# Halves of q and k in an attention kernel: copies by ScalarE, VectorE and GpSimd in place of transfers within SBUF, and another order of the work

## The chip, the cores and the metric

The kernel runs on one core of a Trainium2 chip. The core has TensorE (PE in the profile: matmuls, with PEld for its weight loads), VectorE (DVE), ScalarE (ACT), GpSimd (POOL) and SyncE (SP), which here issues all DMAs; 16 DMA queues move data between HBM, where inputs and outputs lie, and SBUF, the working memory of 128 partitions ("rows" below). Matmuls write to PSUM, here seven buffers of 128x512 f32 and one for the running state. The metric is the device time of one execution in microseconds (us); lower is better.

## The reference

Inputs q, k and v are 4 x 8 x 768 x 64 (batch, heads, sequence, head size). First a retention with decay, then a mixture of four causal attentions over its output, of which each token takes the two with the highest gate:

```python
for t in range(S):
    state = gamma[None, :, None, None] * state + np.einsum('bhd,bhe->bhde', k[:, :, t], v[:, :, t])
    y[:, :, t] = scale * np.einsum('bhd,bhde->bhe', q[:, :, t], state)
...
logits = x @ w_gate
topk = np.argpartition(-logits, K, axis=-1)[..., :K]
...
for e in range(E):
    q = x @ wq[e]
    k = x @ wk[e]
    v = x @ wv[e]
    scores = scale * (q @ k.transpose(0, 2, 1))
    scores = np.where(causal, -1000000000.0, scores)
    scores = scores - scores.max(-1, keepdims=True)
    a = np.exp(scores)
    a /= a.sum(-1, keepdims=True) + 1e-09
    ye = a @ v @ wo[e]
    for kk in range(K):
        mask = topk[:, :, kk] == e
        out += mask[..., None] * w[:, :, kk:kk + 1] * ye
```

Here x is the retention's output as 4 x 768 x 512, and E = 4, K = 2.

## The kernel before

**Stages.** The sequence of each batch is cut into 6 chunks of 128 tokens (24 in all, index g) for the retention, and into 2 halves of 384 tokens (8 in all, index j) for the attention.

- *Retention* (`h1`, `h2`, `kdecay`, `qdecay`; matmuls of lines 477, 481, 536, 542): 64x64 matmuls for four pairs of heads, two heads at a time on the upper and lower 64 rows. Each chunk's q and k come with one load of 512 KB (`qkT_t`, three buffers), k and v in the other layout with a second one (`kv_t`, three buffers). A buffer is free for the next load when the chunk's matmuls and decays are done. The result is split into a rounded part `xh` (ACT) and a rest `xl` (DVE).
- *Projection* (`proj`, lines 577 to 616): for a half j, a pair of experts p and an expert e of it, twelve matmuls (line 592) give q in rows 0 to 63 and k in rows 64 to 127 of one PSUM buffer, 384 tokens wide. ACT takes the rounded part into `k1` (line 597), DVE the rest into `q2` (line 600). Then transfers within SBUF place the parts: the high part of q in both row halves of `q1`, the low part of k in the upper half of `k1` over its high part in the lower half, and the high part of k in the upper half of `k2`. Experts come in pairs, so a transfer holds 64 rows of 2 x 384 values, 192 KB; in the last half (j = 7) each expert has its own, 96 KB.
- *Row maxima* (`mpass`, lines 715 to 737, and `mrow`), *values and gate* (`vgate`, line 634, `gate`, `gate2`).
- *Attention* (`score`, lines 841 and 842): k1 against q1 in 128 rows is (k low + k high) times q high, and k2 against q2 adds k high times q low and, in row 64, the row maximum. ACT takes the exponential into `pt` (line 848), POOL masks the diagonal (line 854) and adds up the denominators (lines 863, 870); `av` (line 889) multiplies with v.
- *Norm and output* (`norm_a`, `norm_b`, `norm_last`, `wout`, line 1015).

**What sets the order.** Each step is recorded by `op` with its engine and what it reads and writes. `ORDER`, a table of numbers, then gives the order in which all steps are written out, and so the order on each engine's queue: engines work their queues in order, and SP issues DMAs in order too, waiting at each for what it depends on. Buffers of a tag are handed out in that order as well. The costs that stand beside the steps now only pick which of a tag's free buffers a step gets.

At the head, `warm` (line 1153) gives PE eight 128x512 matmuls on a tile of zeros, and `idle` (line 1163) six more at two places.

Of the kernel before, what the change touches and what calls it, by code (L numbers as in the profile page):

```python
# [8 lines left out]
F32 = mybir.dt.float32  # L9
# [18 lines left out]
WARM = 8  # L28
IDLE = (2, 4)
# [69 lines left out]
"""  # L99


def act_c(n):
    return 0.17 + n * 0.83e-3


def dve_c(n):
    return 0.15 + n * 1.04e-3
# [140 lines left out]
def tile_retention_moe_attention(  # L248
# [328 lines left out]
    def proj(j, p, e):  # L577
# [35 lines left out]
        for x, rows_ in (("a", up), ("b", low)):  # L613
            move(q1, rows_, k1, up, [(k1, "q", y) for y in es], [(q1, x, y) for y in es])
# [678 lines left out]
```

## Time and profile before

Three runs took 337.05, 338.60 and 338.72 us.

| | |
|---|---|
| median of the runs | 338.60 us |
| the profiled execution's own time | 337.56 us |
| its span in the profile | 335.9 us |
| mean granted clock of TensorE | 0.995 |
| HBM read, written | 29.99 MB, 6.79 MB |
| SP's instructions for moves within SBUF (line 609) | 56 of 192 KB, 16 of 96 KB |

The page gives each engine's busy time, then the span in 40 slices, where each digit is the busy share of a slice in tenths:

```profile
PE   7869979988996799999999999999999999999995
DVE  3832736666624434645664627575634446668753
ACT  2323223421531443244353432353354514547631
POOL 5554322562383695377056894535088733627200
PEclk9999999999997999999999999999999999999999
DMA  7955756654728506565663864442164040443012
```

One slice is 8.4 us. "Idle before" in a group's row is the time in which the engine stood still just ahead of such an instruction, with what ended it; "issue" is idle time that the profile gives no reason for. The chain of waits follows the work that ended last back to the start.

### The profile page before, as it was taken

The numbers are of one execution on the slowest core, as the hardware profiler recorded it, in microseconds if no ns is written. First come the engines' busy times: TensorE is split into PE (matmuls) and PEld (weight loads), VectorE is DVE, ScalarE is ACT, GpSimd is POOL, SyncE is SP. The second block draws the span as 40 slices with busy tenths as digits, with TensorE's granted clock in tenths as the row PEclk, the third lists the DMA queues.
The fourth block names the chain that finished last, engine by engine and source line by source line (L and its number), as shares of the span: only waits on it lengthen the run. The fifth ranks groups of instructions, "written<-read, shape, count | busy, mean of one in ns | idle before, by whom it ended". The sixth has DMA issues, their size and how long they took to land.

```text
span 335.9 us, 11897 instructions
## 1 busy us (share of the span) xinstructions
PE 315.6 (94%) x5060; PEld 278.9 (83%) x5060; DVE 181.2 (54%) x506; ACT 129.0 (38%) x322; POOL 169.0 (50%) x192
## 2 busy tenths in 40 slices
PE   7869979988996799999999999999999999999995
PEld 4669979877985797998999979998998979987773
DVE  3832736666624434645664627575634446668753
ACT  2323223421531443244353432353354514547631
POOL 5554322562383695377056894535088733627200
PEclk9999999999997999999999999999999999999999
DMA  7955756654728506565663864442164040443012
GB/s 264 399 198 182 203 174 198 176 178 158 188 83 237 173 5 193 167 221 146 195 201 91 257 180 136 140 112 88 50 173 100 23 124 24 135 118 91 33 66 95
DMA packets 21642, 50.15 MB, mean 149 GB/s; under 512 B 3186, under 2 KB 8390, under 8 KB 21588
## 3 DMA queue, kind: packets, MB, share of 16 engines
q1 hardware_dynamic: 21588, 49.38, 48.5%
q8 instruction: 40, 0.66, 0.8%
q14 instruction: 14, 0.11, 0.1%
HBM read 29.99 MB, written 6.79 MB: 110 GB/s over the span
## 4 chain that ended last, share of the span: by engine, by line
PE 92%; issue 4%; DMA 1%; DVE 1%; ACT 0%; SPq 0%; ACTq 0%
PE ps L592 20%; PE ps L889 11%; PE ps L634 11%; PE ps L1015 10%; PE ps L841 7%; PE ps L842 6%; PE ps_st L477 5%; PE ps L542 5%; PE ps L729 4%; PE ps L536 3%; PE ps L481 2%; PE ps L715 2%; PE ps L925 2%; DMA qkT_t<-in_qkT_dram 1%; PE ps L728 1%
## 5 line engine op out<-in xcount | busy, mean ns | idle before, releaser
L854 POOL TENSOR_SCALAR_AFFINE_SELECT pt<-pt 128x256 f32<-128x256 f32 x48 | 20.1, 423 | 81.2 <-ACT pt L848 81.0
L848 ACT ACTIVATE pt<-ps 128x384 f32<-128x384 f32 (+2 forms) x112 | 49.4, 494 | 23.8 <-PE ps L842 22.7
L431 POOL TENSOR_TENSOR qd<-qkT_t,tabs 128x512 f32<-128x512 f32 (+1 forms) x23 | 27.9, 1212 | 35.7 <-PE ps L481 16.7
L737 DVE CUSTOM_DVE_ANT_0 scr<-ps,cmask 128x128 bf16<-128x128 f32 (+3 forms) x64 | 30.1, 488 | 27.4 <-PE ps L729 26.9
L592 PE MATMUL ps<-xl,qk_hi 128*128 128x384 f32 x128 | 43.1, 337 | 1.4 <-issue 1.4
L592 PE MATMUL ps<-xh,qk_hi 128*128 128x384 f32 x128 | 43.8, 342 | 0.0
L841 PE MATMUL ps<-q,k 128*128 128x384 f32 (+2 forms) x144 | 43.5, 317 | 0.0
L592 PE MATMUL ps<-xh,qk_lo 128*128 128x384 f32 x128 | 43.1, 337 | 0.0
L842 PE MATMUL ps<-q,k 65*128 65x384 f32 (+2 forms) x144 | 42.4, 312 | 0.0
L889 PE MATMUL ps<-pt,vt 64*64 64x384 f32 (+2 forms) x576 | 42.2, 421 | 0.0
L870 POOL TENSOR_TENSOR ac<-ac,pt 128x256 f32<-128x256 f32 (+2 forms) x32 | 39.9, 1247 | 1.8
L491 DVE TENSOR_TENSOR sblk<-ps_st,tabs 128x256 f32<-128x256 f32 x44 | 18.5, 421 | 41.1 <-PE ps_st L477 37.9
L477 PEld LDWEIGHTS ps_st<-kv_t 64*64 64x64 f32 x704 | 26.6, 136 | 9.5 <-issue 6.6
L477 PE MATMUL ps_st<-kv_t 64*64 64x64 f32 x704 | 30.8, 223 | 3.4 <-issue 2.6
L481 PE MATMUL ps<-qd,sblk 64*64 64x64 f32 x704 | 30.6, 223 | 3.5 <-issue 3.5
L889 PEld LDWEIGHTS ps<-pt,vt 64*64 64x64 f32 x576 | 21.6, 135 | 14.0 <-issue 11.3
L597 ACT ACTIVATE k<-ps 128x384 fp32r<-128x384 f32 x32 | 15.5, 489 | 44.3 <-PE ps L592 44.3
L504 ACT ACTIVATE xh<-ps 128x512 fp32r<-128x512 f32 x24 | 14.3, 598 | 46.4 <-PE ps L481 39.2
L542 PE MATMUL ps<-qkT_t 64*64 64x64 f32 x768 | 27.9, 220 | 2.9 <-issue 2.9
L634 PE MATMUL ps<-vg_hi,xl 128*128 128x260 f32 x96 | 27.3, 284 | 2.2 <-issue 2.2
L542 PEld LDWEIGHTS ps<-qkT_t 64*64 64x64 f32 x768 | 25.9, 136 | 3.6 <-issue 3.3
L841 PEld LDWEIGHTS ps<-q,k 128*128 128x128 f32 x144 | 27.4, 190 | 1.4 <-issue 1.0
(124 smaller groups left out, 778.0 us busy)
## 6 DMA issues: line engine op xcount, KB each, us to landing
qkT_t<-in_qkT_dram SPq DMA_DIRECT2D x24, 512.0 KB
kv_t<-in_kv_dram SPq DMA_DIRECT2D x23, 512.0 KB
q<-k SPq DMA_DIRECT2D x28, 192.0 KB
out_dram<-ot SPq DMA_DIRECT2D x21, 256.0 KB
k<-q SPq DMA_DIRECT2D x14, 192.0 KB
k<-k SPq DMA_DIRECT2D x14, 192.0 KB
fe<-fd SPq DMA_DIRECT2D x28, 96.0 KB
pt<-in_wqk_dram SPq DMA_DIRECT2D x4, 256.0 KB
```

Of the source, the lines that this page charges most:

```text
L477: nc.tensor.matmul(ST[b].t[rows(rt), s * D:(s + 1) * D], kvs(m, 0, s)[rows(rt)], kvs(m, 1, s)[rows(rt)], start=c == 0 and s == 0, stop=Fal ...
L481: nc.tensor.matmul(yo(m, rt, s), SB[m % 2][rows(rt), s], LD[g, 2].t[rows(rt), s, m % 2 * SC:(m % 2 + 1) * SC], start=m % 2 == 0 and s == 0 ...
L542: nc.tensor.matmul(ps.t[rows(rt), a:a + SC], qb.t[rows(rt), 1, s, t], qb.t[rows(rt), 0, s, t], start=True, stop=True)
L592: nc.tensor.matmul(pb.t[:, :HS], ww[:, kt, wsl], xx[:, kt], start=n == 0, stop=n == 11)
L634: nc.tensor.matmul(pb.t[:, :NV + E], xx[:, kt, sl], ww[:, kt], start=n == 0, stop=n == 11)
L737: lambda: nc.vector.tensor_tensor_reduce(scr.t[:, :n1], pb.t[:, :n1], K["cmask"][:, HS + C - n1:], 1.0, mx0.t[:, e, i:i + 1] if prior else ...
L841: nc.tensor.matmul(o, k1.t[:, e, ko:ko + C], q1.t[:, e, q0:], start=True, stop=False)
L842: nc.tensor.matmul(o, k2.t[:65, e, ko:ko + C], q2.t[:65, e, q0:], start=False, stop=True)
L848: lambda es=es, sb=sb, n=n: nc.scalar.activation(pt.t[:, es[0]:es[0] + n, q0:], sb.t[:, :n * w].rearrange("p (e t) -> p e t", e=n), AF.Exp ...
L870: op(eng, cost, lambda: en.tensor_tensor(ac.t[:, :, q0:], ac.t[:, :, q0:], pt.t[:, :, q0:], op=OP.add), r=[(pt, 0), (pt, 1), (ac, "b")], w ...
L889: nc.tensor.matmul(ob.t[e * 64:e * 64 + 64, q0:HS], VTB[kj].t[rr, ko // C, ee * 64:ee * 64 + 64], PTB[j, p, kb].t[rr, e, q0:], start=kb == ...
L1015: nc.tensor.matmul(wb.t, oo[:, sl], ww[:, p], start=n == 0 and p == 0, stop=n == 2 and p == NP - 1)
```

## The change

The parts of a projection are placed by engines. ACT rounds q straight into the upper half of `q1` and k into the lower half of `k1`, one instruction of 64 rows each; DVE writes the rest of q into the upper half of `q2` and the rest of k, read from rows 64 to 127, into rows 0 to 63 of `k1`. Then `turn` makes two copies: the high part of q into the lower half of `q1` (by POOL, in the last half by ACT) and the high part of k into the upper half of `k2` (by ACT). All 72 transfers of line 609 are gone. `PACE` is empty, so its two lines do nothing. `ORDER` is another table, with 1592 numbers in place of 1564.

```diff
+PACE = ()
+QP = True
+KP = False
...
 ORDER = """
-0 5 1 108 109 87 110 4 7 2 3 23 26 8 22 24 6 27 25 28 11 13 9 12 10 38 34 39 29 36 14 30 42 88 44 48 46 89 37 52 31 45
...
+1 5 2 4 108 9 3 6 13 17 11 7 8 14 19 88 12 24 0 26 25 18 28 10 42 27 15 29 66 31 34 16 30 71 43 44 38 75 32 39 45 40
...
+            if g in PACE:
+                R.ops[-1].deps.add(R.ops[-2])
...
-        op("ACT", act_c(HS), lambda: nc.scalar.activation(k1.t[:, e], pb.t[:, :HS], AF.Copy), r=[(pb,)],
-           w=[(k1, "q", e), (k1, "h", e)])
+        up, low = slice(0, 64), slice(64, 128)
+        op("ACT", act_c(HS), lambda: nc.scalar.activation(q1.t[up, e], pb.t[up, :HS], AF.Copy), r=[(pb,)],
+           w=[(q1, "a", e)])
+        op("ACT", act_c(HS), lambda: nc.scalar.activation(k1.t[low, e], pb.t[low, :HS], AF.Copy), r=[(pb,)],
+           w=[(k1, "h", e)])
         op("DVE", dve_c(HS),
-           lambda: nc.vector.tensor_tensor(q2.t[:, e], pb.t[:, :HS], k1.t[:, e], op=OP.subtract),
-           r=[(pb,), (k1, "q", e), (k1, "h", e)], w=[(q2, "x", e), (q2, "l", e)])
+           lambda: nc.vector.tensor_tensor(q2.t[up, e], pb.t[up, :HS], q1.t[up, e], op=OP.subtract),
+           r=[(pb,), (q1, "a", e)], w=[(q2, "x", e)])
+        op("DVE", dve_c(HS),
+           lambda: nc.vector.tensor_tensor(k1.t[up, e], pb.t[low, :HS], k1.t[low, e], op=OP.subtract),
+           r=[(pb,), (k1, "h", e)], w=[(k1, "q", e)])
         each = j == NJ - 1
         if not e and not each:
             return
         es = [e] if each else range(2)
-
-        def move(d, dr, s, sr, r, w):
-            a, b = es[0], es[-1] + 1
-            op("SP", 0.4, lambda: nc.sync.dma_start(d.t[dr, a:b].bitcast(F32), s.t[sr, a:b].bitcast(F32)),
-               r=r, w=w, nbytes=167000 * len(es))
-
-        up, low = slice(0, 64), slice(64, 128)
-        for x, rows_ in (("a", up), ("b", low)):
-            move(q1, rows_, k1, up, [(k1, "q", y) for y in es], [(q1, x, y) for y in es])
-        move(k1, up, q2, low, [(q2, "l", y) for y in es], [(k1, "q", y) for y in es])
-        move(k2, up, k1, low, [(k1, "h", y) for y in es] + [("k2ones",)], [(k2, "x", y) for y in es])
+        a, b = es[0], es[-1] + 1
+        n = len(es) * HS
+
+        def turn(pool, d, s, r, w):
+
+            if pool:
+                op("POOL", pool_c(n), lambda: nc.gpsimd.tensor_copy(d(), s()), r=r, w=w)
+            else:
+                op("ACT", act_c(n), lambda: nc.scalar.activation(d(), s(), AF.Copy), r=r, w=w)
+
+        turn(QP and not each, lambda: q1.t[low, a:b], lambda: q1.t[up, a:b], [(q1, "a", y) for y in es],
+             [(q1, "b", y) for y in es])
+        turn(KP and not each, lambda: k2.t[up, a:b], lambda: k1.t[low, a:b], [(k1, "h", y) for y in es] + [("k2ones",)],
+             [(k2, "x", y) for y in es])
```

The lines of the kernel after the table move by 7, and after `proj` by 16: line 477 of before is 484, line 592 is 599, line 1153 is 1169.

What the table moves is seen in each engine's queue. First PE at the very start of the program, before: the last of the eight warm-up matmuls (`wu` is the tile of zeros), then the turn of the first chunk's k (line 398) and its first retention steps.

```order
L1153 LDWEIGHTS wu_153
L1153 MATMUL ps_1_140<-wu_153 128x512
L398 MATMUL ps_6_145<-ident_159,qkT_t_0_63 64x64 x16
L542 MATMUL ps_0_139<-qkT_t_0_63 64x64 x16
L477 MATMUL ps_st_0_146<-kv_t_0_66 64x64 x8
L542 MATMUL ps_2_141<-qkT_t_1_64 64x64
L536 MATMUL ps_1_140<-am_0_70,kv_t_0_66 64x64
```

PE at the start, after the change:

```order
L1305 UNCONDITIONAL_BRANCH
L549 MATMUL ps_0_139<-qkT_t_0_63 64x64 x16
L405 MATMUL ps_1_140<-ident_159,qkT_t_0_63 64x64 x16
L549 MATMUL ps_3_142<-qkT_t_1_64 64x64
L543 MATMUL ps_2_141<-am_0_70,kv_t_0_66 64x64
```

The retention now opens the queue. The warm-up stands further down, behind the first chunk's steps:

```order
L484 MATMUL ps_st_0_146<-kv_t_0_66 64x64
L488 MATMUL ps_2_141<-qd_0_69,sblk_1_155 64x64
L1179 LDWEIGHTS wu_153
L1179 MATMUL ps_5_144<-wu_153 128x512
L1169 LDWEIGHTS wu_153
L1169 MATMUL ps_6_145<-wu_153 128x512
```

One of line 1179, eight of line 1169 and four of line 1179 follow each other there; one more of line 1179 stands a little ahead.

Next SP's queue, about where the thirteenth to fifteenth load of `kv_t` stand, before (`q1<-k1`, `k1<-q2` are moves; `md`, `fe` belong to the row maxima and the norm):

```order
L609 DMA q1_2_78<-k1_0_82 64x768
L385 DMA kv_t_0_66<-in_kv_dram 128x1024
L771 DMA q2_0_79<-md_1_136 1x768
L943 DMA fe_0_126<-fd_0_137 64x384
L377 DMA qkT_t_1_64<-in_qkT_dram 128x1024
L609 DMA k1_4_86<-q2_1_80 64x768
L377 DMA qkT_t_2_65<-in_qkT_dram 128x1024
L385 DMA kv_t_2_68<-in_kv_dram 128x1024
L385 DMA kv_t_1_67<-in_kv_dram 128x1024
```

After the change, the same three loads of `kv_t`:

```order
L390 DMA kv_t_1_67<-in_kv_dram 128x1024
L959 DMA fe_0_126<-fd_0_137 64x384 x2
L382 DMA qkT_t_2_65<-in_qkT_dram 128x1024
L959 DMA fe_0_126<-fd_0_137 64x384
L785 DMA md_1_136<-mt_1_106 6x128
L787 DMA q2_0_79<-md_1_136 1x768
L390 DMA kv_t_2_68<-in_kv_dram 128x1024
L382 DMA qkT_t_1_64<-in_qkT_dram 128x1024
L1048 DMA out_0_dram<-ot_0_127 128x512
L390 DMA kv_t_0_66<-in_kv_dram 128x1024
```

The moves are gone, and other short transfers and an output stand between the loads.

Last, POOL's queue in the second half sequence, before (`qd` is the decayed q of a chunk, line 416 scales a loaded k):

```order
L416 TENSOR_TENSOR kv_t_0_66<-kv_t_0_66,tabs_162 128x512
L353 TENSOR_TENSOR wo_lo_152<-pt_4_113,wo_hi_151 128x512
L431 TENSOR_TENSOR qd_0_69<-qkT_t_1_64,tabs_162 128x512
L416 TENSOR_TENSOR kv_t_1_67<-kv_t_1_67,tabs_162 128x256
L431 TENSOR_TENSOR qd_0_69<-qkT_t_2_65,tabs_162 128x512
```

After the change:

```order
L423 TENSOR_TENSOR kv_t_0_66<-kv_t_0_66,tabs_162 128x512
L625 COPY q1_0_76<-q1_0_76 64x768
L438 TENSOR_TENSOR qd_0_69<-qkT_t_1_64,tabs_162 128x512
L423 TENSOR_TENSOR kv_t_2_68<-kv_t_2_68,tabs_162 128x512
L438 TENSOR_TENSOR qd_0_69<-qkT_t_2_65,tabs_162 128x512
L423 TENSOR_TENSOR kv_t_1_67<-kv_t_1_67,tabs_162 128x256
L625 COPY q1_1_77<-q1_1_77 64x768
```

The copies of q stand between the decays and the scalings that the retention reads.

116 rows, old and new, of the table ORDER are left out of this document.

## The prediction

> **What bounds the kernel now.** I read the page first: how busy is the busiest engine, and what else lies on the chain that ends last?
>
> ```profile
> span 335.9 us, 11897 instructions
> PE 315.6 (94%) x5060; PEld 278.9 (83%) x5060; DVE 181.2 (54%) x506; ACT 129.0 (38%) x322; POOL 169.0 (50%) x192
> ...
> q1 hardware_dynamic: 21588, 49.38, 48.5%
> q8 instruction: 40, 0.66, 0.8%
> ...
> PE 92%; issue 4%; DMA 1%; DVE 1%; ACT 0%; SPq 0%; ACTq 0%
> ```
>
> TensorE is busy for 315.6 of 335.9 us, so 20.3 us are all that can go unless its work shrinks, and the change leaves its 5060 matmuls alone. The chain holds 1% of DVE and none of ACT: hardly anything on the other engines is waited for. The largest thing beside PE is "issue", time with no visible cause. The waits of PE say how much, the chain says when:
>
> ```profile
> PE ps L481 <- issue: 3.5, 3, 1.5
> PE ps L542 <- issue: 2.9, 2, 2.2
> PE ps_st L477 <- issue: 2.6, 1, 2.6
> PE ps L634 <- issue: 2.2, 1, 2.2
> PE ps L592 <- issue: 1.4, 1, 1.4
> ```
>
> ```profile
> 13.12 0.72 issue
> ...
> 17.59 2.60 issue
> ```
>
> Eight stalls (columns: total, times, longest), 3.5 + 2.9 + 2.6 + 2.2 + 1.4 = 12.6 us. The two of the chain, 3.3 us, lie in the head; six, 9.3 us, lie later. What are they? Queue q8 carries 40 instruction packets, 0.66 MB, so 16 KB each; PE and PEld have 10,120 instructions, so a packet is a block of some 253. The DMA view of the window 101.0 to 103.5, which holds L634's stall of 2.2 us, has
>
> ```profile
> q8 instruction: 1, 0.02, 2.3%
> ```
>
> One block of code came just there: PE had run out of instructions. Stretches of about a block show when that happens (columns: PE, PEld, DVE, ACT, POOL busy with counts, clock, DMA share, GB/s):
>
> ```profile
> 73.50:77.90 4.40, 4.40 (x143) 3.51 (x136) 3.91 (x12) 1.25 (x3) 2.65 (x3) 1.00 0.90 326
> 98.40:101.20 2.80, 2.80 (x138) 2.48 (x131) 1.07 (x4) 0.84 (x2) 1.27 (x3) 1.00 0.91 277
> 145.90:150.20 4.30, 4.30 (x141) 4.23 (x130) 2.29 (x5) 2.09 (x6) 4.13 (x5) 1.00 0.65 190
> 166.00:168.80 2.80, 2.80 (x132) 2.34 (x136) 1.26 (x3) 1.25 (x3) 0.41 (x1) 1.00 0.42 106
> 103.00:108.70 5.70, 5.22 (x127) 4.56 (x126) 1.32 (x4) 0.77 (x2) 1.21 (x2) 0.70 0.92 266
> ```
>
> The first two ran 270 to 280 instructions in 4.4 and 2.8 us with DMA 0.90 busy, and PE stalled behind each (L592's 1.4 us, L634's 2.2). The next two ran as many as fast, with DMA at 0.65 and 0.42: no stall. **A stall needs a quick block (64-row matmuls of the recurrence) and full DMA queues together.** The change touches both. The last row is what follows the 2.2 us stall: a granted clock of 0.70 over 5.22 us of work, so 0.30 x 5.22 = 1.6 us lost besides.
>
> **Removed: the moves.** By the page's DMA issues,
>
> ```profile
> qkT_t<-in_qkT_dram SPq DMA_DIRECT2D x24, 512.0 KB
> kv_t<-in_kv_dram SPq DMA_DIRECT2D x23, 512.0 KB
> q<-k SPq DMA_DIRECT2D x28, 192.0 KB
> ...
> k<-q SPq DMA_DIRECT2D x14, 192.0 KB
> k<-k SPq DMA_DIRECT2D x14, 192.0 KB
> ```
>
> 56 of 192 KB go, and the 16 smaller ones of the last half sequence (half the bytes each): 12.3 of 49.4 MB, a quarter. No PE wait of the trace names them, so their landing time is worth nothing by itself. The loads stay, and they are most of what stood ahead of the block of L634's stall: two of 512 KB and two moves, by SP's order. A stall is what sticks out of a fetch over the block that covers it: here 2.2 us over 2.8, a wait of 5.0. If the wait goes with the bytes ahead, a quarter off is 1.25 us, about half of the stall.
>
> **Moved: PE's order.** I cut PE's two orders into stretches of 254 instructions and priced each by the trace's mean start-to-start times of the same matmuls (an estimate). Beyond the head, 13 stretches pass in under 4.6 us before, 9 after: the recurrence is spread between projections. The 13 had 9.3 us of stalls, 0.72 each. Nine at half of that leave 9 x 0.36 = 3.2. Bounds: 0 (all like the row at 166.0) and 9 x 0.72 = 6.5. I take 3.2, a gain of **6.1**; and the lost clock, **1.6**, comes back, since the stall ahead of it is halved.
>
> **Moved: the warm-up.** Before, eight warm-up matmuls run while PE waits for data; afterwards they stand behind the first real work.
>
> ```profile
> 1.06 3.59 PE L1153 MATMUL ps<-wu 128*128 128x512 bf16 x8 [1.06 <-POOL wu L1103]
> 5.90 1.15 PE L398 MATMUL ps<-ident,qkT_t 64*64 64x64 f32 x32 [1.24 <-DMA qkT_t<-in_qkT_dram]
> ...
> 10.32 1.25 PE L1163 MATMUL ps<-wu 128*128 128x512 bf16 x5
> 12.39 0.27 PE L477 MATMUL ps_st<-kv_t 64*64 64x64 f32 x1 [0.82 <-DVE kv_t L416]
> ```
>
> The eight took 0.45 us each, the same matmul later 0.25: PE starts at about half speed. Now real work pays that from 5.90 on, for as long as the eight took: 3.59 / 2 = 1.8 us. Real work up to the first step that needs the second chunk's k and v (at 12.39) is 10.32 - 5.90 = 4.4 us; behind it come 14 fillers, 3.5 us, in place of 5. So that step starts at 5.9 + 4.4 + 1.8 + 3.5 = 15.6, 3.2 later. Its load has 0.9 MB more ahead of it (SP's order), at 326 GB/s 2.8 us, which runs beside that. The stall of 0.72 just behind is then covered; the one of 2.60 I keep. Head: **+2.5**, bounds 0 (waits swallow it) and +4.4 (all its real work at half speed). The Trainium skill ("TensorE: Matmul & The Clock Gate", section "Part 1: The HAM clock gate") says that an idle array stands at half clock and is released after about 3.4 us of sustained work; that speaks against this part, and agrees with the 3.59 us here. It also has the clock fall only after an idle window of that length; here a stall of 2.2 us stood before the fall. By the rule the fall would have another cause and its 1.6 us stay, which makes the sum below 335.4.
>
> **Added: engine work.** Prices (line, tile and shape, count | busy, mean ns), ACT, then DVE and POOL:
>
> ```profile
> L597 ACT ACTIVATE k<-ps 128x384 fp32r<-128x384 f32 x32 | 15.5, 489 | 44.3 <-PE ps L592 44.3
> ...
> L352 ACT ACTIVATE qk_hi<-pt 128x512 fp32r<-128x512 f32 x4 | 2.3, 624 | 0.0
> L761 ACT ACTIVATE q<-ps 1x384 fp32r<-1x384 f32 x4 | 1.8, 478 | 0.1
> ```
>
> ```profile
> L600 DVE TENSOR_TENSOR q<-ps,k 128x384 fp32r<-128x384 f32 x32 | 17.3, 551 | 19.4 <-ACT k L597 19.4
> ```
>
> ```profile
> L870 POOL TENSOR_TENSOR ac<-ac,pt 128x768 f32<-128x768 f32 x12 | 22.0, 1830 | 0.6
> L854 POOL TENSOR_SCALAR_AFFINE_SELECT pt<-pt 128x256 f32<-128x256 f32 x48 | 20.1, 423 | 81.2 <-ACT pt L848 81.0
> ```
>
> One row of 384 costs ACT as much as 128 rows (478, 489), so splitting an eviction by halves doubles it: 32 more at 0.49, 15.6 us. ACT's 14 copies of 64x768 (k into k2) lie between 0.62 (512 columns) and 1.25 (twice that); along the two ACT rows, 0.135 for 128 columns, 0.89. Eight copies of 64x384 at 0.49. Sum 15.6 + 12.5 + 3.9 = 32 us: ACT goes from 38% to 48%. DVE gets 32 x 0.551 = 17.6, 54% to 59%. POOL's 14 copies of 64x768 lie between a mask of 256 columns (0.42) and a two-input add of 768 (1.83); with one input I go by three masks, 1.27: 17.8 us, 50% to 55%. All of it runs beside PE: ACT waits 44.3 us for projections and POOL 81.0 us for exponentials. A projection's PSUM buffer is held about 1 us longer (one more eviction on each engine), and q and k are ready some 3 us after it. New waits are 0 where that cover lasts; I put **+0.5**, bounds 0 and 9 (the third rival).
>
> **Switches of PE's tile mode** rise from 67 to 76 by the order. The nearest row is the weight load's idle time at attention's mode, 0.17 us each:
>
> ```profile
> PEld ps L889 <- issue: 11.3, 65, 0.3
> ```
>
> Nine between 0 and 0.17, I take 0.1: **+0.9**. The last 25 us have the same instructions in nearly the same order: 0.
>
> **Sum:** -6.1 - 1.6 + 2.5 + 0.9 + 0.5 = -3.8 us. The profiled execution took 337.56 us (1.66 around its span), so 333.8. It stood 1.0 below the median of 338.6, inside the runs' 337.05 to 338.72; I don't correct for that.
>
> **The rivals.**
> - *All later stalls go.* For it: the row with DMA at 0.42 ran a block in 2.8 us without one, and three quarters of 0.91 are 0.68, near the 0.65 where none came. Against: a load is issued when a recurrence step frees its buffer, so beside the quick blocks. 337.56 - 9.3 - 1.6 + 2.5 + 0.9 = 330.1.
> - *The loads do it, not the moves*, and the change does not do what it says. Each quick block keeps its 0.72: 9.3 - 6.5 = 2.8 won, no clock back; 337.56 - 2.8 + 2.5 + 0.9 + 0.5 = 338.7. For it: 1024 KB of loads stood against 384 KB of moves.
> - *POOL's copies make PE wait: slower.* POOL works in order. A copy waits for both of ACT's halves of q, and behind it stand the decay of q for the recurrence, the scaling of a loaded k, and the masks that attention needs. At 1.83 us a copy that nothing covers delays PE by its own length; five of the 14 are 9.2 us: 333.8 - 0.5 + 9.2 = 342.5. From four on it is slower than before. For it: at 145.9 POOL is busy 4.13 of 4.30 us. Against: its 81.0 us of waits for ACT.
>
> **How the numbers follow.** Forecast (some stalls stay): 0.43, 333.8. All go: 0.25, 330.1. The loads do it: 0.17, 338.7. POOL: 0.15, 342.5. Half a per cent of 338.6 is 1.7 us, about what a measurement of this kernel can tell from no change. So faster 0.43 + 0.25 = 0.68, same 0.17, slower 0.15. The range leaves out POOL's case and the lowest tail: 329.0 to 340.0.
>
> **What would show it.** Right: q1 near 37 MB; PE's issue waits at 5 to 7 us, 2 to 3 of them in the head; the clock at 1.00 from 20 us on; the second chunk's first step near 15.6 us; ACT near 161 us busy. Wrong: PE waiting for POOL's or ACT's q and k; issue waits still near 12 us with q1 down a quarter; a head at half speed beyond 10 us.

## The result and the profile after

| | before | changed kernel |
|---|---|---|
| median of the runs | 338.66 us (337.05 to 341.67) | 328.95 us (328.32 to 330.60) |
| ratio, 95% interval | | 0.971 [0.963, 0.979] |
| the profiled execution's own time | 337.56 us | 330.60 us |
| a second profiled execution (run e5 below) | | 328.74 us, span 327.0 |

It is faster by 2.9%, 9.7 us; 333.8 was predicted, and the median lies 0.05 below the range's lower end. The profiled execution is the slowest of its four, so the profiles differ by 7.0 us only; the second profile is nearer to the median. Here and below, medians are over all runs of a kernel, ratios over its fast runs alone, those within 1.5% of its quickest.

The page after, as far as the prediction used it:

```profile
PE 315.1 (96%) x5060; PEld 279.2 (85%) x5060; DVE 200.7 (61%) x538; ACT 162.2 (49%) x376; POOL 180.4 (55%) x206
...
q1 hardware_dynamic: 15828, 36.79, 34.1%
q8 instruction: 39, 0.64, 0.7%
...
PE 92%; DMA 4%; DVE 1%; issue 1%; SPq 0%; ACT 0%; ACTq 0%
```

PE has the same work; "issue" on the chain has gone from 4% to 1%, and the DMA queues' share from 48.5 to 34.1%. The chain's DMA has grown from 1 to 4%: it is loads of k and v in the head, the last of them the second chunk's (start, us):

```profile
8.54 7.38 DMA kv_t<-in_kv_dram
```

All waits of PE above 0.3 us:

```profile
PE ps L549 <- DMA qkT_t<-in_qkT_dram: 4.9, 1, 4.9
PE ps L650 <- issue: 1.9, 1, 1.9
PE ps L1179 <- DVE xl L514: 1.8, 1, 1.8
```

(Columns: total, times, longest, in us.) All three stand in the head, before 29 us: the first load, the next stretch's code, and one filler. Of the later stalls for code none is left, and none of the copies is waited for. Where the time went is read best from PE's busy time by stage (us, PE, PEld, DVE, ACT, POOL, clock, DMA share, GB/s); first before:

```profile
0.00:40.00 40.00, 33.55 (x797) 28.84 (x798) 19.46 (x47) 11.69 (x25) 21.07 (x32) 1.00 0.73 250
40.00:115.00 75.00, 65.79 (x1331) 59.80 (x1330) 40.07 (x112) 23.82 (x62) 32.68 (x37) 0.98 0.59 172
```

then the changed kernel:

```profile
0.00:40.00 40.00, 30.43 (x691) 26.67 (x695) 18.97 (x37) 10.35 (x22) 20.48 (x30) 0.96 0.71 236
40.00:115.00 75.00, 75.00 (x1530) 68.90 (x1523) 52.62 (x138) 39.01 (x90) 44.07 (x50) 1.00 0.40 132
115.00:200.00 85.00, 85.00 (x1334) 77.15 (x1333) 50.26 (x141) 42.09 (x99) 56.80 (x59) 1.00 0.35 114
```

The head lost 3.1 us of busy time and some clock; 40 to 115 us won 9.2 us of it and the clock's 0.02, and PE is never idle there. The head's 0.96 is a fall behind its 1.9 us stall (28.6 to 32.0 us at half clock, 1.7 us); the second profile, with a stall of 1.1, has 1.00.

Why do the quick blocks not stall? Three of them, the quickest, in the changed kernel:

```profile
96.70:99.60 2.90, 2.90 (x142) 2.22 (x135) 1.90 (x4) 2.79 (x7) 2.90 (x4) 1.00 0.11 20
141.20:143.40 2.20, 2.20 (x131) 2.01 (x129) 2.17 (x5) 0.50 (x2) 0.20 (x1) 1.00 0.18 60
217.50:219.60 2.10, 2.10 (x134) 1.93 (x134) 0.99 (x3) 0.48 (x3) 1.95 (x3) 1.00 0.13 47
```

They are as quick as any before, but the queues are nearly idle beside them; over all nine the share is 0.09 to 0.55. Before, the five longest of the later stalls (1.4 to 2.2 us) stood behind blocks with 0.85 to 0.98.

### The profile page after: what moved, and what is told of

Same layout as the page of the kernel before. It is cut to its first block, busy times and chain, and to the rows that moved or that the text cites. A ratio compares the mean times of both kernels' runs of the same rounds, so it can differ in the third digit from the quotient of the medians.

```text
span 328.7 us, 11866 instructions
## 1 busy us (share of the span) xinstructions
PE 315.1 (96%) x5060; PEld 279.2 (85%) x5060; DVE 200.7 (61%) x538; ACT 162.2 (49%) x376; POOL 180.4 (55%) x206
## 3 DMA queue, kind: packets, MB, share of 16 engines
q1 hardware_dynamic: 15828, 36.79, 34.1%
## 4 chain that ended last, share of the span: by engine, by line
PE 92%; DMA 4%; DVE 1%; issue 1%; SPq 0%; ACT 0%; ACTq 0%
PE ps L599 21%; PE ps L905 11%; PE ps L650 11%; PE ps L1031 11%; PE ps L857 7%; PE ps L858 6%; PE ps_st L484 5%; PE ps L549 5%; DMA kv_t<-in_kv_dram 4%; PE ps L745 4%; PE ps L731 2%; PE ps L488 2%; PE ps L543 2%; PE ps L941 2%; PE ps L744 1%
## 5 line engine op out<-in xcount | busy, mean ns | idle before, releaser
L753 DVE CUSTOM_DVE_ANT_0 scr<-ps,cmask 128x256 bf16<-128x256 f32 (+3 forms) x64 | 30.2, 486 | 35.9 <-PE ps L745 35.7
L599 PE MATMUL ps<-xh,qk_hi 128*128 128x384 f32 x128 | 44.6, 348 | 0.0
L905 PE MATMUL ps<-pt,vt 64*64 64x384 f32 (+2 forms) x576 | 41.7, 415 | 0.0
L438 POOL TENSOR_TENSOR qd<-qkT_t,tabs 128x512 f32<-128x512 f32 (+1 forms) x23 | 28.6, 1243 | 22.1 <-PE ps L488 18.1
L484 PE MATMUL ps_st<-kv_t 64*64 64x64 f32 x704 | 29.4, 221 | 0.6 <-DVE kv_t L423 0.3
L498 DVE TENSOR_TENSOR sblk<-ps_st,tabs 128x256 f32<-128x256 f32 x44 | 18.5, 421 | 18.6 <-PE ps_st L484 17.7
L484 PEld LDWEIGHTS ps_st<-kv_t 64*64 64x64 f32 x704 | 24.9, 134 | 5.7 <-issue 3.6
L605 ACT ACTIVATE q<-ps 64x384 fp32r<-64x384 f32 x32 | 15.4, 480 | 28.0 <-PE ps L599 27.9
L488 PE MATMUL ps<-qd,sblk 64*64 64x64 f32 x704 | 29.2, 221 | 0.0
```

What stands on the lines that cost most here:

```text
L484: nc.tensor.matmul(ST[b].t[rows(rt), s * D:(s + 1) * D], kvs(m, 0, s)[rows(rt)], kvs(m, 1, s)[rows(rt)], start=c == 0 and s == 0, stop=Fal ...
L488: nc.tensor.matmul(yo(m, rt, s), SB[m % 2][rows(rt), s], LD[g, 2].t[rows(rt), s, m % 2 * SC:(m % 2 + 1) * SC], start=m % 2 == 0 and s == 0 ...
L599: nc.tensor.matmul(pb.t[:, :HS], ww[:, kt, wsl], xx[:, kt], start=n == 0, stop=n == 11)
L753: lambda: nc.vector.tensor_tensor_reduce(scr.t[:, :n1], pb.t[:, :n1], K["cmask"][:, HS + C - n1:], 1.0, mx0.t[:, e, i:i + 1] if prior else ...
L905: nc.tensor.matmul(ob.t[e * 64:e * 64 + 64, q0:HS], VTB[kj].t[rr, ko // C, ee * 64:ee * 64 + 64], PTB[j, p, kb].t[rr, e, q0:], start=kb == ...
```

## The experiments

Two things changed together, the copies and the order. The question is which of them took the stalls away, and which the time.

**Copies at the old order (e1).** The order of before, with the copies at the places of the evictions and moves:

```diff
 ORDER: that of before, where a projection's steps read
-  ACT k1 | DVE q2 | SP q1 up, SP q1 low, SP k1 up, SP k2 up
+  ACT q1 up, ACT k1 low | DVE q2 up, DVE k1 up | POOL q1 low, ACT k2 up
```

> The copies by ACT, DVE and POOL stand at the places that the evictions and moves have in the order of before; the rest of that order stays, so the quick blocks of PE code stay where they were. Theory B (the moves' bytes held up PE's code): the six later stalls, 9.3 us, fall below 3 us and the low clock behind the longest goes with them, the head stays that of before, so 327 to 332 us. Theory O (the order did it: fewer quick blocks, in other places): the later stalls stay at 7 us or more, 335 to 339 us. If POOL's copies make PE wait where the order was not made for them, PE waits for POOL or ACT appear that the changed kernel does not have, and the time is above what the stalls alone give.

Measured: 339.9 us, 0.999 [0.996, 1.003] of before: nothing won. Yet most later stalls are gone (PE's longer waits; L488 is the recurrence, L941 the norm):

```profile
PE ps L488 <- issue: 2.5, 1, 2.5
PE ps_st L484 <- issue: 1.5, 1, 1.5
PE ps L488 <- POOL qd L438: 1.4, 2, 0.7
...
PE ps L941 <- issue: 0.9, 1, 0.9
...
PE ps L781 <- DVE mx L753: 0.8, 2, 0.7
...
PE ps L731 <- DVE k L613: 0.5, 1, 0.5
PE ps L774 <- ACT k L607: 0.5, 1, 0.5
```

Behind 40 us 3.4 us of issue waits stay, of 9.7 (the prediction's 9.3 and 0.4 of L536). PE's order is the same in both kernels, so its 5060 matmuls can be set side by side one by one: at number 2000 (103.1 us against 110.3) the copies' kernel is 7.2 us ahead. Then comes the stall of 2.5, from 103.4 to 105.9 us. The stretch ahead of it, and what lies behind it:

```profile
98.40:103.40 5.00, 4.67 (x145) 4.08 (x137) 4.65 (x10) 1.67 (x4) 3.25 (x3) 1.00 0.61 193
...
106.00:108.00 2.00, 2.00 (x13) 1.88 (x14) 0.62 (x1) 0.60 (x1) 1.15 (x2) 0.50 0.10 31
108.00:110.00 2.00, 2.00 (x14) 1.78 (x15) 0.36 (x3) 1.67 (x5) 1.92 (x3) 0.50 0.64 207
110.00:112.00 2.00, 2.00 (x80) 2.00 (x82) 0.44 (x3) 0.06 (x1) 0.60 (x1) 0.55 0.14 55
```

That is six microseconds at half clock. The block ahead of the stall (256 instructions in 4.3 us, from 99.1 us on) is quick, but its queues are not full in the mean: 0.61 in the row, where the row at 145.9 us of before had 0.65 and no stall. They were near idle from 99 to 101 us (0.22 and 0.01) and at 0.96 from 101 to 105, and the next packet of code came from 103.5 to 104.4. So the prediction's condition of full queues, taken as a mean over a block, misses the longest stall that is left. From 126 us on small waits take the rest (for row maxima, k and x by VectorE and ACT, and code once): it is 1.9 us ahead there and 2.3 behind at the end. So theory B comes close for the stalls (3.4 us, where it said below 3) and fails for the clock and the time.

**Moves at the new order (e2).** The old projection code at the new table, the four moves right behind their VectorE step.

```diff
 ORDER: the new one, where a projection's steps read
-  ACT q1 up, ACT k1 low | DVE q2 up, DVE k1 up | POOL q1 low, ACT k2 up
+  ACT k1 | DVE q2, SP q1 up, SP q1 low, SP k1 up, SP k2 up
```

> The moves within SBUF are back, each group of four right behind its VectorE step in the new order; evictions are those of before. Theory B: the later stalls come back, 3 us or more of issue waits behind 40 us, 333 to 340 us. Theory O: under 1 us of issue waits behind 40 us, 328 to 331 us. Against both: SP waits at each move in a new place and so issues the loads later; then PE shows waits for loads (qkT or kv) that the changed kernel does not have, and the time says little on either.

Measured: 360.4 us, 1.061 [1.057, 1.065].

```profile
PE ps L729 <- DMA k<-q: 9.5, 2, 9.0
PE ps L542 <- DMA qkT_t<-in_qkT_dram: 6.0, 1, 6.0
PE ps L842 <- DMA q<-md: 5.7, 3, 2.7
PE ps L715 <- DMA q<-k: 2.6, 2, 2.0
...
PE ps L889 <- issue: 1.4, 1, 1.4
...
PE ps L925 <- issue: 0.4, 1, 0.4
```

1.8 us of issue waits are left behind 40 us, between what the two theories said: most of them are gone at this order with the moves in place, too. But now PE waits for the moves themselves, and for `q<-md`, the row maxima, which go by DRAM in the same queues. The moves stand at places that I chose in SP's queue, so the 21 us are no clean price of them; that they land too late at these places is clear, and whether better places exist in the new order was not tested.

**The new order with traffic that nobody waits for (e3, e4).**

```diff
+        for x in range(4):
+            op("SP", 0.4, lambda x=x: nc.sync.dma_start(DZ[x][:, a:b], q1.t[up, a:b].bitcast(F32)), nbytes=-1)
+
         turn(QP and not each, lambda: q1.t[low, a:b], lambda: q1.t[up, a:b], [(q1, "a", y) for y in es],
```

(`range(8)` in the second run; the queues of PE, ACT, DVE and POOL are row by row those of the changed kernel.)

> The changed kernel with 72 more transfers of the moves' size and shape (64 rows of 768 or 384 values), issued by SP where the moves would be, from q1 into an unused DRAM buffer; nobody waits for them and all else is word for word the changed kernel. Theory B: 3 to 6.5 us of issue waits come back behind 40 us, 332 to 336 us. Theory O: under 1 us of them, within 1 us of the changed kernel's 329.

> As the run with 72 unused transfers, with twice as many. Theory B: issue waits behind 40 us grow beyond those with 72, to 6 us or more, 335 to 342 us. Theory O: the new order has no block of code that is both quick and late, still under 1.5 us of issue waits, within 1.5 us of 329; if loads land late instead, PE waits for qkT or kv and not for issue.

Measured: with 72, four runs from 335.1 to 344.7 us, median 339.8; the two quicker ones alone (335.1 and 336.3) give 0.988 [0.984, 0.992] of before, 1.7% over the changed kernel's 0.971. With 144, 380.8 us, 1.117 [1.109, 1.124]. Both theories are wrong on where most of the loss lies. With 72 (the profile is that of the slowest run, 344.7 us, so its waits are not those of the two quicker ones) and with 144:

```profile
PE ps L870 <- DMA q<-md: 5.0, 4, 2.7
PE ps L662 <- issue: 1.9, 1, 1.9
PE ps L495 <- POOL qd L445: 1.8, 1, 1.8
...
PE ps L743 <- ACT on L935: 0.7, 1, 0.7
```

```profile
PE ps L873 <- DMA q<-md: 19.5, 4, 5.4
PE ps L559 <- DMA qkT_t<-in_qkT_dram: 8.1, 2, 5.2
PE ps L920 <- POOL pt L885: 3.0, 1, 3.0
...
PE ps L746 <- ACT on L938: 1.0, 1, 1.0
```

Behind 40 us no wait is put down to code, though one quick block ran beside full queues, with 72 and with 144:

```profile
229.00:231.20 2.20, 2.20 (x136) 2.03 (x140) 1.01 (x3) 0.58 (x3) 2.05 (x4) 1.00 0.98 368
```

```profile
253.60:255.70 2.10, 2.10 (x134) 1.93 (x134) 0.99 (x3) 0.48 (x3) 1.95 (x3) 1.00 1.00 378
```

The waits of 0.75 and 1.03 us just behind these are put down to ACT, which had been done for 0.5 and 0.8 us. By their place they are waits for code. Both stand at the same number of PE's queue, where a new block of code begins (see the last section), and so does the 1.4 us that e2 has there as issue. All three end 1.4 to 1.5 us after a packet of queue q8 has landed; the nine waits of before for code end 1.2 to 1.6 us after one. The changed kernel's first profile, with the same block beside queues at 0.13, shows no wait there. So in the new order, too, bytes beside a quick block bring a stall, here of 0.75 to 1.4 us. But the two conditions together are not enough: with 144 a quick stretch at 154.5 us beside queues at 0.96 has no stall behind it. What the bytes cost most with 144, and in the slowest run with 72, is the row maximum's way through DRAM. The clock falls behind the longest waits (with 144, those of 2.9 to 5.4 us); the mean clock of the two profiles is 0.98 and 0.945.

**One quick block of the old order broken up (e9).** In e1's queue of PE, three scores are moved into the stretch at 103 us:

```diff
 L484, L488 (first half of the chunk)
+L857, L858 (two scores, 4 matmuls)
 L549, L543
+L857, L858 (one score, 2 matmuls)
 L488 (second half)
-L857, L858 (the same three scores)
```

> The run with copies at the old order, with three scores (six matmuls, about 1 us) moved from behind the second chunk's steps at 103 us to between them, so that the block of code there takes longer. Theory F (that order's last big loss is code that comes late: the 2.5 us stall at 103.4 us and the half clock of 105.9 to 111.5 us behind it): the stall falls by 1 us or more, and where it stays under 1.5 us the half clock goes too; 1 to 5 us faster than the run with copies at the old order, 0.985 to 0.997 of before. Theory W (the copies' own waits are what that order lost): the stall moves or shrinks and the time stays within 0.3% of before.

Measured: the median of twelve runs is 338.2 us, where before, run beside them, took 338.4. The ratio of 0.992 [0.987, 0.996] rests on the four quickest runs alone (332.9 to 337.3 us), so the times by themselves do not show a gain. The trace shows what the edit did. At the old stall's place (number 4005 of PE's instructions in both) PE now stands still for 1.1 us, not 2.5; 0.9 us comes one block later; and the half clock is gone:

```profile
106.00:108.00 2.00, 1.81 (x39) 1.47 (x39) 0.86 (x4) 0.98 (x2) 1.39 (x2) 1.00 0.35 143
```

Set side by side matmul by matmul, e9's trace is 0.2 us behind e1's ahead of this place, 3.1 us ahead just behind it, and 2.6 us shorter at the end (spans 335.4 and 338.0). So theory F holds for this stall and for the clock in the profiled execution, which is one of the four quickest. In the other eleven the mean clock lies between 0.984 and 0.999, so in most of them the clock fell somewhere; where is not on record. The 2.5 us and the half clock behind it were one stretch's work; the rest of what the old order loses is not touched by this edit.

**The head (e5 to e8, e10, e13).** The changed kernel again as a base, then its head in steps: warm-up first on PE; the second chunk's k and v loaded earlier; both; then VectorE's, ACT's and GpSimd's queues.

```diff
 e6, PE:   +L1169 wu x8, ahead of the first L549   (and L1119, zeroing wu, first on POOL)
 e7, SP:   +kv_t (second chunk) behind the first kv_t, ahead of seven loads of weights
 e8:       e6 and e7
 e10:      e8, and DVE: +L423 kv_t, +L514 xl ahead of L358 vg_lo; ACT: L511 xh third
 e13:      e10, and POOL: +L438 qd ahead of three L358 splits
```

> The changed kernel unaltered, as the base of the three head runs on this chip. Both theories: 0.965 to 0.978 of before, no issue waits behind 40 us.

> The changed kernel with its eight warm-up matmuls back in front of all real work on PE (and the zeroing of their tile first on POOL); nothing else moves. Theory W (the first real work at half speed is what the head lost): 1.5 to 2 us faster than the changed kernel on this chip. Theory K (the head waits for the second chunk's k and v, whose load was put behind 1.6 MB of other loads): the first matmuls end sooner and PE waits longer for that load, within 0.5 us of the changed kernel, or slower, since the fillers behind now leave a longer gap.

> The changed kernel with the load of the second chunk's k and v moved ahead of the weights' loads in SP's queue; the four pieces for values and gate, then the pieces for q and k follow. Theory K: the second chunk's first step moves from 16.4 us to 12 to 14 us, 2 to 4 us faster than the changed kernel. Theory W: under 1 us of gain. A new wait could take its place: the pieces of the weights for q and k land some 1.6 us later, and their splits with them.

> Both head edits together. Theory K with W: the two gains add, 3.5 to 6 us faster than the changed kernel, about 323 to 326 us, since the head is then near that of before. Theory W alone: no more than the run with the warm-up first. If the head's stalls for code grow with the faster start, under 2 us of gain.

> The run with warm-up first and the second chunk's load early, and besides in VectorE's queue that chunk's decay of k and the first rest of x ahead of the weights' splits, and ACT's first rounding of x as its third instruction. Theory Q (the head waited for VectorE's queue: the decay of k stood behind a split, a fill and two others, 12.5 to 16.5 us): the second chunk's first step starts near 12.5 us, not 16 to 18, and the whole is 2 to 4 us faster than the changed kernel, 0.958 to 0.966 of before. Theory L (the head is held by its loads: some 9 MB up to 30 us): the wait goes to the weights' splits and the values' matmuls, under 1 us of gain, 0.968 to 0.975.

> The run with VectorE's and ACT's head order changed, and besides the second chunk's decay of q ahead of the weights' splits in GpSimd's queue, where it stood behind three of them (13.2 to 16.0 us) and made PE wait 5.1 us. Theory Q (queues in order held the head, one behind the other): that wait of PE falls under 1 us, the second chunk's steps run from 12.7 us, and 2 to 4 us go: 0.958 to 0.966 of before. Theory L (the loads hold the head): PE then waits as long for values' weights or for the next chunk's loads, 0.968 to 0.975.

| | median us | ratio, interval | largest wait of PE in the head |
|---|---|---|---|
| e5 changed kernel | 329.25 | 0.971 [0.967, 0.976] | first load 4.7, filler 1.8 |
| e6 warm-up first | 329.04 | 0.968 [0.964, 0.973] | DVE kv_t L423, 3.7 |
| e7 load early | 330.64 | 0.974 [0.969, 0.978] | first load 5.1, DVE kv_t L423 2.3 |
| e8 both | 330.79 | 0.974 [0.970, 0.979] | DVE kv_t L423, 5.5 |
| e10 and VectorE, ACT | 329.61 | 0.974 [0.970, 0.978] | POOL qd L438, 5.1 |
| e13 and GpSimd | 328.33 | 0.973 [0.967, 0.978] | DVE sblk L498, 2.2 |

None of the five edits can be told from the changed kernel. Where an edit took away a wait, the next queue in order took its place. In e8 VectorE's queue holds (start, us, instruction):

```profile
15.50 0.81 DVE L358 TENSOR_TENSOR qk_lo<-pt,qk_hi 128x512 fp32r<-128x512 f32 x1
16.23 0.68 DVE L514 SCALAR_TENSOR_TENSOR xl<-ps,xh 128x512 fp32r<-128x512 f32 x1
16.83 1.15 DVE L423 TENSOR_TENSOR kv_t<-kv_t,tabs 128x512 f32<-128x512 f32 x1
```

The decay of k (L423), which here waits for no load, stands behind a split of weights and the rest of x. The profiles of e6 and e13 are shorter (spans 325.0 and 325.6 against 327.0), by less than these runs separate. In e6 the wait of 3.7 us cost the clock as well (0.66 from 15 to 20 us). Theories W, K and Q each fall as the one holder of the head. That the loads hold it (DMA 0.98 to 1.04 busy from 5 to 15 us in e5, e6 and e13 alike) would fit, but was not tested by a run with fewer bytes.

**Which engine copies (e11, e12, e14, e15).**

```diff
-QP = True
-KP = False
+QP = True, KP = True      # e11: both copies on POOL
+QP = False, KP = False    # e12, e15: both on ACT; e14: that and e13's head
```

> The changed kernel with both copies of a pair of experts on POOL (the high part of k too). ACT loses 14 x 0.84 = 11.8 us, POOL gains about 14 x 0.82 = 11.5 us, to 58%. Theory C (the copies lie beside PE and the engine does not matter): within 1.5 us of the changed kernel. Theory P (POOL works in order and its copies delay masks and decays): PE waits for POOL or for a k of POOL appear, 2 to 5 us slower.

> The changed kernel with both copies on ACT (the high part of q too). POOL loses 11.5 us, ACT gains 11.8, to 53%. Theory C: within 1.5 us of the changed kernel. Theory P: faster by the waits that POOL's copies cost, 1 to 3 us; if ACT is the tighter engine, 1 to 4 us slower, with PE waits for exponentials.

> The same with both copies of a pair on ACT. Theory C (the engine of the copies does not matter): within 1 us of the run with GpSimd's head order. If ACT is the better place, up to 1.5 us faster than that.

> Both copies on ACT, head as in the changed kernel, as the base. 0.965 to 0.973 of before.

Measured: 328.64 us, 0.971 [0.967, 0.975]; 327.83, 0.969 [0.964, 0.973]; e14 328.23, 0.972 [0.966, 0.977]; e15 328.67, 0.974 [0.967, 0.980]. POOL at 59% or ACT at 53% makes no difference that these runs can tell: theory C. In the new order the copies lie beside PE, and in none of these profiles does PE wait for one.

## Why the prediction was off

- **What bounds the kernel:** right. The time came from PE's stalls for code between 40 and 115 us and from the clock behind one of them.
- **The later stalls, "nine at half of that leave 9 x 0.36 = 3.2": this step failed.** Nothing was left: the rival "all later stalls go" was the right case. Its 330.1 is 1.2 above the median; the 0.9 for switches, which never showed, is most of that. (That it is near the profiled 330.6 is chance: that execution lost 1.7 us to a fall of the clock that the sum does not have.) The mean of 0.72 was spread over quick blocks as if each stalled alike. Five of the six stood behind blocks with the queues at 0.85 to 0.98, the two longest behind two quick blocks in a row; the new order has its nine blocks beside queues at 0.09 to 0.55. The argument against that rival, that a load is issued "beside the quick blocks", was not tried on the new order. The halving by bytes was about right for the old order (3.4 of 9.7 left in e1), but here the order's own effect comes on top (1.8 of 9.7 left in e2, with the moves in place).
- **The lost clock, 1.6:** came back, as its stall went; the reading under which it stays (335.4) did not come true. e1 and e9 show the link: a stall of 2.5 us is followed by 6 us at half clock, stalls of 1.1 and 0.9 at that place by none. That a halved stall brings the clock back was a premise without a row; before has two other stalls of 2.2 and 2.6 us without a fall. The size is that of one execution. In the 52 other runs of before on record the mean clock has a median of 0.985, where the profiled one had 0.995; the changed kernel's ten have 0.992 to 1.000. A difference of 0.010 over 336 us is 3.4 us, so an ordinary run of before had more clock to win back than the 1.6.
- **The head, +2.5:** 2.7 us of busy time up to 40 us in the second profile (33.55 less 30.86), 3.1 and 1.7 of clock in the first. Right in size, but by another path, so the size is in part luck. The second chunk's first step came at 16.7, not 15.6 (the 16.4 in e7's expectation is the end of the filler ahead of it). Its load, which the prediction had running beside the rest, was in at 15.9 only and stands on the chain, and VectorE's decay of k followed it. The warm-up's return to the front in e6 gave no gain that can be measured.
- **Engine prices:** ACT 162.2 us busy (161 predicted), VectorE 200.7 (181.2 and the 17.6 are 198.8), GpSimd 180.4 (169.0 and the 17.8 are 186.8). The rows of the copies: 0.84 us on ACT (0.89 predicted), and on POOL 0.82, where three masks had given 1.27:

```profile
L627 ACT ACTIVATE k<-k 64x768 fp32r<-64x768 f32 x14 | 11.8, 841 | 0.3
L625 POOL CAST q<-q 64x768 fp32r<-64x768 f32 x14 | 11.5, 820 | 22.9 <-ACT q L605 22.4
```

- **New waits, +0.5, and switches, +0.9:** not seen. No copy is waited for, and from 40 to 200 us PE shows no idle time that nine more switches could have made. (The weight load's idle time that the prediction took as its nearest row fell from 11.3 to 8.7 us.) At the old order the waits were real, some 4 us.
- **The sum:** -9.7 for the stalls, -1.6 for the clock and +2.7 for the head are -8.6; the second profile is 8.8 shorter than the one of before. The other 0.9 of the 9.7 is which executions were profiled, and how an ordinary run splits into stalls and clock is open.

So neither part does it alone as it was run here. The copies free the queues, but at an order that was not made for them their waits and one stall with its half clock give it back; the new order with the moves, at the places that I chose, waits for the moves. Together copies and order give 2.9%. What the order would be worth with well-placed moves stays open.

## What to carry to other kernels

When transfers are replaced by copies, search the order again before judging: the same copies were worth 0% at the old order and 2.9% at the new. A stall for code is priced block by block, from the DMA share beside that block and the block next to it in the new order, not by a mean over all; and the share of a whole block can still hide the microseconds in which the code had to come, as in e1. Taking away one wait in a head where several engines work in order only names the next one.

## What was not expected of the hardware

- The clock's fall has a sharp price: PE standing still for 2.5 us cost another 2.7 at least (half clock from 106 to 111.5 us). A stall of 1.9 us was followed by a fall in one run (the changed kernel's first profile) and by none in another (e11), 1.3 us (e12) by none. In before itself the stall of 2.2 us at 101 us was followed by a fall, and those of 2.6 us at 17.6 and 2.2 us at 41.7 were not (clock 1.00 behind both). So the length of a stall alone does not decide; what else does is open. The Trainium skill ("TensorE: Matmul & The Clock Gate", section "Part 1: The HAM clock gate") gives a window of about 3.4 us; stalls well below it were enough here, and the half clock lasted 3.4 us (28.6 to 32.0) and longer.
- PE's stalls for code lie at fixed places, 254 instructions apart: counted in the trace of before, the five longest behind 40 us stand at PE's instructions 1717, 2476, 2984, 3748 and 4001, which are 3, 2, 3 and 1 times 254 apart, within 3. Counted together with the 86 records of PE's sequencer, all seven behind 40 us stand whole multiples of 256 apart, to the instruction. By that count the waits of 0.75 us (e3), 1.03 us (e4) and 1.4 us (e2) all stand at number 7873, which is 15 times 256 behind the stall of 1.5 us at 4033 in before.
- A copy of 64 rows by 768 f32 costs GpSimd no more than ScalarE, 820 and 841 ns.
